# Constant rows of the later q-k buffers by DMA from one small template, at the beginning of an attention and expert kernel

## The chip, the cores and the metric

The kernel runs on one core of one Trainium2 chip. Its time is the device time of one launch in microseconds (us): 778.45 us as the median of three runs (775.94 to 778.54).

## The reference

What is computed is causal attention over 8 batches of 8 heads (576 positions, head size 64) with a bias made of a running sum, and then a layer of eight experts. Each token goes to one expert by a greedy assignment with a capacity of 576 tokens per expert. Cut to what matters:

```python
scores = scale * q @ k.T                      # 8 x 8 heads, 576 x 576
cum    = cumsum(maximum(s, 0))
scores = where(causal, -1e9, scores + minimum(-(cum_i - cum_j), 0))
attn   = exp(scores - max); attn /= attn.sum() + 1e-9
x      = attn @ v                             # 4608 tokens x 512
logits = x @ w_gate                           # 8 experts
# greedy assignment by descending logit, at most 576 tokens for an expert
out[mask_e] = relu(x[mask_e] @ w1[e]) @ w2[e] # for each expert e
```

## The kernel before, in words

The attention works on groups: a group is half the heads of one batch, that is two pairs of heads, and there are 16 groups. A pair is done in three passes on TensorE. The S pass (method `spass`) makes the scores only to find each row's maximum: TensorE writes a tile into one of three `pss` buffers, VectorE adds the mask and takes the maximum (line 471, called a max step below, ten to a pair, each followed by a read of the accumulator). The maxima become two more rows of the q-k buffer: ScalarE and GpSimd split them (lines 518, 520 and 522), TensorE transposes them (524), and a small DMA puts them in place (530). The transposed pass (method `sts`, lines 544 to 547) computes the transposed scores with the maxima subtracted; ScalarE takes the exponential into `P` (555) and GpSimd makes the remainder `R` (557). The third pass multiplies with v (lines 618 to 620).

Numbers are kept as a high and a low half in 16 bits, so a group's q and k need eight copies in a buffer `QK` of 128 partitions. Four such buffers (QK_91 to QK_94 in the instruction lists) are used in turn by the groups 0, 1, 2, 3, 4 and so on. In each, partitions 64 to 69 hold rows for the bias: three that change with the data and come by small DMAs ("aux" rows, line 397), and parts that stay the same in the whole run. These constant rows, and zeros between the halves (lines 297 and 298), are written once per buffer, in `consts`. For buffers 0 and 1 VectorE writes the constant rows (line 285, two instructions for a buffer); buffers 2 and 3 get a copy of buffer 1's by DMA from GpSimd's queue (line 290).

The method `load` brings a group in: four loads of q and k into a `raw` buffer (line 382; two `raw` buffers in turn, 87 and 88), the high half by ScalarE (409), the low half by VectorE (411), moves between partitions by DMA (416), and the aux rows (397). In its list `fresh` stand the waits for the constant rows and zeros of the group's buffer. For group 1 the list also holds `self.moved`, the two DMAs that copy buffer 1's rows.

The order of all instructions is set by a planner (class `Plan`). Each task has an engine, a guessed duration, what it needs, and a priority; the planner plays the program through with its guesses and writes every engine's instructions down in the order that comes out. Each engine then works its list strictly in order, and a waiting instruction holds up all that stand behind it; the DMA issues of the queues SP and GpSimd too. A task with `alt` may go to a second engine.

Before the first group's data is there, TensorE runs 70 matmuls on zeros that nobody reads (line 735, called warm-up below). They stand in its list by priority too, most ahead of the first S pass and the rest between its matmuls.

After the attention follow the router (assignment) and the experts, each with its own plan.

Of the kernel before, what the change touches and what calls it, by code (L numbers as in the profile page):

```python
# [10 lines left out]
F16 = mybir.dt.float16  # L11
# [3 lines left out]
OP = mybir.AluOpType  # L15
# [201 lines left out]
class Attention:  # L217
# [30 lines left out]
    def consts(self):  # L248
        nc, c, pl = self.nc, self.c, self.pl
        g = nc.gpsimd  # L250
        T = lambda shape, dt, name: c.tile(shape, dt, name=name)
        k = self.k = {}
# [19 lines left out]
        for c, v0, rows in ((0, C1, ((5, 0.0), (3, C3), (2, C2), (1, C1))), (1, PSHIFT, ((5, -C1),))):  # L272
            v = self.vec[64:96, c:c + 1]
            P(("vec", c, 0), 0.1, lambda v=v, v0=v0: g.memset(v, v0), -99)
            for n, (below, val) in enumerate(rows):
                P(("vec", c, n + 1), 0.2, lambda v=v, below=below, val=val: g.affine_select(
                    v, v, pattern=[[0, 1]], base=-below, channel_multiplier=1, compare_op=OP.is_ge, fill=val), -99, [("vec", c, n)])
        zrow = self.mZ.bitcast(F16)[64:70, None, 0:HB // 2].to_broadcast([6, 4, HB // 2])
        for i in range(4):
            t = self.r["QK"].slots[i][0]  # L280
            p0 = -97 if i == 0 else 2 * i - 5.6
            rows, made = t[64:70, 0], []
            if i < 2:
                for c in (1, 0):
                    made.append(pl.add("v", 0.85, lambda rows=rows, c=c: nc.vector.tensor_scalar(
                        rows[:, c].rearrange("p r (h c) -> p (r h) c", h=2), zrow, self.vec[64:70, c:c + 1], None,
                        op0=OP.add), [k["vec", 0, 4], k["vec", 1, 1], k["mZ"]], prio=p0 if c or i else -94, lock=True))
            else:

                made.append(pl.add("p", 0.9, lambda rows=rows: nc.gpsimd.dma_start(rows, self.r["QK"].slots[1][0][64:70, 0]),  # L290
                                   self.rows1 + [k["QK", 1]], prio=-20, kb=62))
                self.moved.append(made[0])
            k["row", i] = made
            if i == 1:
                self.rows1, self.moved = made, []
            x = t.rearrange("p a t r c -> p (a t r) c")[:, :, S:OH]
# [66 lines left out]
    def load(self, g):  # L363
# [21 lines left out]
        fresh = [k["QK", g]] if g < 4 else []  # L385
        if g == 1:
            fresh = fresh + self.moved

        if g == 0:
# [15 lines left out]
        for a, z in parts:  # L405
# [3 lines left out]
            hi = [pl.add("a", dur, lambda t=t, a=a, z=z: act(part(A_, 1, t, t, a, z), raw.t[:, t, a:z], AF.Copy, scale=QS),  # L409
                         [ld[r, t] for r in range(a, z)] + fresh[:1], prio=t0 - 5 + off + t / 10, uses=[raw, QK]) for t in range(2)]  # L410
            lo = [pl.add("v", 0.15 + n * S / 960, lambda t=t, a=a, z=z: stt(
# [1060 lines left out]
```

## Time and profile before

| | |
|---|---|
| median of three runs | 778.45 us (775.94 to 778.54) |
| the profiled execution | 777.66 us, of which the span of its instructions 775.6 us |
| TensorE (PE) busy | 722.0 us, 93% of the span |
| VectorE (DVE) busy | 598.2 us, 77% |
| ScalarE (ACT) busy | 391.7 us, 50% |
| GpSimd (POOL) busy | 335.3 us, 43% |
| mean granted clock of TensorE | 0.964 of full |

The shares are averages over stages with different limits: the attention takes about the first 318 us, then the router and the experts. The row of the granted clock in 40 slices shows three places below full speed: slices 2 and 3 of the attention's beginning, slices 17 and 18 between attention and experts, and the last. TensorE's granted clock is given as a share of 2.4 GHz, so 0.5 is 1.2 GHz.

In the rows by windows come, after the stretch and its length, the busy us of PE, PEld (weight loads), DVE, ACT and POOL with the count of instructions, the granted clock (PEclk), the mean busy share of the 16 DMA engines, and GB/s. In a timeline the first number is the start in us from the span's start, the second the time the merged instructions take; in brackets stands how long the engine had been idle before and what released it.

### The profile page before, as it was taken

To read this page: it belongs to the slowest core of one execution; us is meant where nothing else is said; L and a number is where in the kernel's file an instruction comes from. 1 tells how busy PE (TensorE), PEld (TensorE's weight loads), DVE (VectorE), ACT (ScalarE), POOL (GpSimd) and SP (SyncE) were. 2 spreads that over 40 slices of the span, in tenths; PEclk is the share of its full clock that TensorE was granted. 3 is DMA by queue.
4 is the path that set the end of the run, shared out by engine and by line. 5 is a ranking of instruction groups with operands and counts; after the bars stand their busy time and mean duration, and the time that the engine had idled before them with its cause. 6 is when DMAs were issued, how large, how long until landed. Compare 5 with 4: busy or idle time off the path is not lost.

```text
span 775.6 us, 22590 instructions
## 1 busy us (share of the span) xinstructions
PE 722.0 (93%) x8726; PEld 454.9 (59%) x8726; DVE 598.2 (77%) x2014; ACT 391.7 (50%) x794; POOL 335.3 (43%) x428
## 2 busy tenths in 40 slices
PE   9789999999999999628998999999999999999995
PEld 3457788787888888416644544545445454454542
DVE  7889999999999996678895877969788795380110
ACT  3548888888888878405334323324244232461110
POOL 7648988788878988102032041140412224202011
PEclk9679999999999999858999999999999999999998
DMA  7897768686776511106157376394845639851000
GB/s 233 195 213 202 220 175 250 172 241 196 209 203 171 156 35 64 63 35 204 42 167 200 110 113 180 129 222 133 190 156 155 187 105 262 228 180 48 15 28 34
DMA packets 89733, 118.72 MB, mean 153 GB/s; under 512 B 39246, under 2 KB 55758, under 8 KB 89614
## 3 DMA queue, kind: packets, MB, share of 16 engines
q1 hardware_dynamic: 83116, 97.82, 46.1%
q0 software_dynamic: 5952, 19.00, 8.1%
q8 instruction: 68, 1.11, 0.6%
q10 hardware_dynamic: 558, 0.47, 0.2%
q14 instruction: 39, 0.32, 0.1%
HBM read 71.67 MB, written 19.10 MB: 117 GB/s over the span
## 4 chain that ended last, share of the span: by engine, by line
PE 54%; issue 19%; DVE 13%; DMA 5%; POOL 4%; ACT 2%; SPq 1%; POOLq 0%; ACTq 0%; DVEq 0%
PE psm L1293 13%; PE psm L1379 10%; DVE pss L471 5%; PE pst L545 4%; PE pst L544 4%; PE pss L502 3%; PE po L618 3%; PE po L620 2%; PE po L619 2%; POOL out_dram L1352 2%; POOL xg L1226 2%; PE psn L1297 2%; PE po L735 2%; PE pss L681 2%; DMA xg<-xs,ids 1%
## 5 line engine op out<-in xcount | busy, mean ns | idle before, releaser
L557 POOL TENSOR_TENSOR R<-P 128x512 f16<-128x512 f32 (+1 forms) x221 | 218.9, 1016 | 26.9 <-ACT P L555 25.2
L1293 PE MATMUL psm<-xT,w1p 128*128 128x512 f16 (+1 forms) x876 | 193.1, 353 | 1.3 <-DMA xT<-xg 0.8
L1379 PE MATMUL psm<-w2p,hT 128*128 128x512 f16 x768 | 174.4, 379 | 0.0
L555 ACT ACTIVATE P<-pst 128x512 f32<-128x512 f32 (+1 forms) x224 | 119.9, 555 | 25.0 <-PE pst L547 10.3
L1297 PE MATMUL psn<-xT,w1p 128*128 128x64 f16 x768 | 129.7, 193 | 0.0
L471 DVE CUSTOM_DVE_ANT_0 pss<-pss,mS 128x512 f32<-128x512 f32 (+3 forms) x256 | 122.7, 506 | 9.0 <-PE pss L502 8.0
L1293 PEld LDWEIGHTS <-w1p 128*128 128x128 f16 x876 | 79.2, 98 | 80.0 <-issue 1.9
L1352 POOL DMA_INDIRECT out_dram<-y,ids x40 | 39.8, 995 | 198.7 <-ACT y L1390 169.6
L1379 PEld LDWEIGHTS <-hT 128*128 128x128 f16 x768 | 69.0, 98 | 80.3 <-issue 4.4
L1226 POOL DMA_INDIRECT xg<-xs,ids x40 | 43.6, 1089 | 167.3 <-DVE ids L1184 67.3
L618 PE MATMUL po<-V,P 128*128 128x65 f16 x960 | 113.8, 196 | 1.4 <-DVE xp L649 1.0
L620 PE MATMUL po<-V,R 128*128 128x65 f16 x960 | 114.0, 194 | 0.4 <-POOL R L557 0.4
L619 PE MATMUL po<-Vl,P 128*128 128x64 f16 x960 | 113.6, 193 | 0.0
L544 PE MATMUL pst<-QK 70*128 70x64 f16 (+4 forms) x512 | 108.5, 252 | 1.2 <-ACT P L555 0.7
L545 PE MATMUL pst<-QK 128*128 128x64 f16 (+4 forms) x512 | 107.8, 251 | 0.0
L619 PEld LDWEIGHTS <-P 128*128 128x128 bf16 x960 | 90.0, 100 | 9.1 <-issue 2.8
L618 PEld LDWEIGHTS <-P 128*128 128x128 bf16 x960 | 90.4, 98 | 5.9 <-issue 1.8
L1313 ACT ACTIVATE hT<-psm 128x512 f16<-128x512 f32 x64 | 38.2, 597 | 108.1 <-PE psm L1293 88.3
L620 PEld LDWEIGHTS <-R 128*128 128x128 f16 x960 | 89.9, 97 | 0.6 <-POOL R L557 0.6
L1390 ACT ACTIVATE y<-psm 128x512 f32<-128x512 f32 x32 | 19.1, 597 | 122.0 <-PE psm L1379 108.1
L502 PE MATMUL pss<-QK 67*128 67x512 f16 (+3 forms) x256 | 72.6, 307 | 4.7 <-DVE mr L471 2.4
L1297 PEld LDWEIGHTS <-w1p 128*128 128x128 f16 x768 | 67.7, 98 | 1.3
(221 smaller groups left out, 1443.4 us busy)
## 6 DMA issues: line engine op xcount, KB each, us to landing
QK<-QK SPq DMA_DIRECT2D x120, 144.0 KB
wst<-in_w_dram SPq DMA_DIRECT2D x32, 512.0 KB
wst<-in_w_dram SPq DMA_DIRECT2D x64, 256.0 KB
raw<-in_q_dram SPq DMA_DIRECT2D x32, 288.0 KB
raw<-in_k_dram SPq DMA_DIRECT2D x32, 288.0 KB
rv<-in_v_dram SPq DMA_DIRECT2D x32, 288.0 KB
xs<-xp SPq DMA_DIRECT2D x32, 256.0 KB
xs<-xp SPq DMA_DIRECT2D x8, 128.0 KB
```

Source lines behind the costliest of these rows:

```text
L471: return pl.add("v", dur, lambda: nc.vector.tensor_tensor_reduce(ps(), ps(), mask, 1.0, init() if init else -3e38, OP.add, OP.max, mr.t[:, ...
L502: nc.tensor.matmul(ps.t[:, :n], F()[:, q0:q0 + 128], F()[:, k0:k0 + n], start=True, stop=True)
L544: nc.tensor.matmul(ps[:, c0:c0 + n], F()[:, ks:ks + 128], F()[:, q:q + n], start=True, stop=False)
L545: nc.tensor.matmul(ps[:, c0:c0 + n], G()[:, ks:ks + 128], G()[:, q:q + n], start=False, stop=not diag)
L555: e = pl.add("a", n / 1200 + 0.171, lambda: nc.scalar.activation(P.t[:, c0:c0 + n], ps.t[:, :n], AF.Exp, scale=1.0 / YS), [x] + fresh, pri ...
L557: sub = lambda eng: eng.tensor_tensor(R.t[:, c0:c0 + n], P.t[:, c0:c0 + n], strided_hi(P.t)[:, c0:c0 + n], op=OP.subtract)
L618: nc.tensor.matmul(o[:, i], H[:, c:c + 128], V.t[:, pr, sl], start=f, stop=False)
L619: nc.tensor.matmul(o[:, i, 0:64], H[:, c:c + 128], Vl.t[:, pr, sl], start=False, stop=False)
L620: nc.tensor.matmul(o[:, i], R.t[:, c:c + 128], V.t[:, pr, sl], start=False, stop=l)
L1293: nc.tensor.matmul(ps[:, tiles[0]:tiles[-1] + 1] if len(tiles) > 1 else ps[:, tiles[0]], lhs(f, c, a), xT.t[:, tiles[0]:tiles[-1] + 1, 4 * ...
L1297: nc.tensor.matmul(pt.t[:, 64 * f:64 * f + 64], lhs(f, c, a), xT.t[:, 4, 4 * b + c, 0:64], start=s, stop=e)
L1379: nc.tensor.matmul(py.t, hT.t[:, f, a, 128 * i:128 * i + 128], w2p.t[:, f, b], start=f == 0 and k == 0, stop=f == 7 and k == 2)
```

## The change

Only the constants and the loads of the attention are touched. A template tile `rowc` is made: for each of the two kinds of rows 320 columns on six partitions, by one VectorE instruction each. Buffers 1, 2 and 3 get their constant rows from it: two DMAs per buffer on GpSimd's queue, each repeating the 320 columns eight times. The two VectorE instructions that wrote buffer 1's rows are gone, and so are the DMAs that copied them on. The list of group 1 no longer holds the waits for those copies, and the high halves of groups 1 to 3 no longer wait for their buffer's constant rows.

```diff
+        self.rowc = self.c.tile([128, 2, 320], F16, name="rowc")
+        k["rowc"] = [pl.add("v", 0.2, lambda c=c: nc.vector.tensor_scalar(
+            self.rowc[64:70, c], self.mZ.bitcast(F16)[64:70, 0:320], self.vec[64:70, c:c + 1], None, op0=OP.add),
+            [k["vec", 0, 4], k["vec", 1, 1], k["mZ"]], prio=-93, lock=True) for c in (1, 0)]
         for i in range(4):
...
-            if i < 2:
+            if i < 1:
                 for c in (1, 0):
                     made.append(pl.add("v", 0.85, lambda rows=rows, c=c: nc.vector.tensor_scalar(
...
-                made.append(pl.add("p", 0.9, lambda rows=rows: nc.gpsimd.dma_start(rows, self.r["QK"].slots[1][0][64:70, 0]),
-                                   self.rows1 + [k["QK", 1]], prio=-20, kb=62))
-                self.moved.append(made[0])
+                for c in (1, 0):
+                    made.append(pl.add("p", 0.9, lambda rows=rows, c=c: nc.gpsimd.dma_start(
+                        rows[:, c].rearrange("p r (n c) -> p (r n) c", c=320),
+                        self.rowc[64:70, c:c + 1, :].to_broadcast([6, 8, 320])), k["rowc"],
+                        prio=-92 if i == 1 else -20, kb=31))
...
         fresh = [k["QK", g]] if g < 4 else []
-        if g == 1:
-            fresh = fresh + self.moved
...
-                         [ld[r, t] for r in range(a, z)] + fresh[:1], prio=t0 - 5 + off + t / 10, uses=[raw, QK]) for t in range(2)]
+                         [ld[r, t] for r in range(a, z)] + (fresh[:1] if g == 0 else []), prio=t0 - 5 + off + t / 10,
+                         uses=[raw, QK]) for t in range(2)]
```

The planner plays the changed tasks through anew, so the whole attention comes out in another order. Lines below the new ones are numbered two higher after the change.

VectorE, from the low halves of group 0 (QK_91) to the first max steps of its first pair. Before:

```order
L258 MEMSET V_96 128x18
L411 SCALAR_TENSOR_TENSOR QK_91<-raw_87,QK_91 128x576 x4
L285 TENSOR_SCALAR QK_92<-mZ,vec 6x2560
L471 ISA pss_122,mr_105<-pss_122,mS 128x128
L471 ISA mr_105 128x1
```

And after the change:

```order
L258 MEMSET V_97 128x18
L413 SCALAR_TENSOR_TENSOR QK_91<-raw_87,QK_91 128x576 x4
L413 SCALAR_TENSOR_TENSOR QK_92<-raw_88,QK_92 128x2x576 x2
L473 ISA pss_122,mr_105<-pss_122,mS 128x128
L473 ISA mr_105 128x1
```

The constant row of buffer 1 (QK_92) is gone from this place, and the two low halves of group 1, which stood between the max steps of group 0's second pair, now stand ahead of the first max step.

Of TensorE's 70 warm-up matmuls 57 instead of 55 stand ahead of the first S pass.

TensorE, the end of the S pass of group 0's second pair (buffer QK_91). Before, the transposed pass (L544) follows at once:

```order
L502 MATMUL pss_123<-QK_91 128x512
L486 LDWEIGHTS QK_91
L486 MATMUL pss_124<-QK_91 128x512
L486 LDWEIGHTS QK_91
L486 MATMUL pss_124<-QK_91 128x512
L544 LDWEIGHTS QK_91
L544 MATMUL pst_126<-QK_91 128x512
```

After the change matmuls of group 1's S pass (QK_92) stand between, from the first of these rows to the last:

```order
L488 MATMUL pss_124<-QK_91 128x512
L504 LDWEIGHTS QK_92
L504 MATMUL pss_122<-QK_92 128x128
L504 LDWEIGHTS QK_92
L504 MATMUL pss_123<-QK_92 128x256
...
L504 LDWEIGHTS QK_92
L504 MATMUL pss_122<-QK_92 128x256
L546 LDWEIGHTS QK_91
L546 MATMUL pst_126<-QK_91 128x512
```

Seven of the ten tiles of group 1's first pair are now ahead of the transposed pass of group 0's first pair.

GpSimd, from the mask `mU` to the split of the first pair's maxima (mp_110), after the change (before, none of the DMAs and no memset of a QK buffer stood ahead of mp_110):

```order
L261 AFFINE_SELECT mU<-mU 64x64
L295 DMA QK_92<-rowc 6x8x320 x2
L295 DMA QK_93<-rowc 6x8x320 x2
L295 DMA QK_94<-rowc 6x8x320 x2
L301 MEMSET QK_92 128x8x128
L301 MEMSET QK_93 128x8x128
L813 IOTA W 128x8
L301 MEMSET QK_94 128x8x128
...
L828 AFFINE_SELECT tri<-on 128x128
L524 TENSOR_TENSOR mp_110<-ms_108,mp_110 128x10
```

Six DMA issues and three memsets have moved ahead of the router's constants and of mp_110; four selects of the router went behind it.

On SP's queue the moves of group 1 (QK_92) now come ahead of the loads of group 2 (raw_87), which stood before them:

```order
L418 DMA QK_92<-QK_92 64x2x576 x2
L418 DMA QK_91<-QK_91 64x576
L418 DMA QK_92<-QK_92 64x2x576 x2
L442 DMA rv_89<-in_v_dram 128x576
L398 DMA QK_92<-auxk 3x2x576 x2
L418 DMA QK_91<-QK_91 64x576
L386 DMA raw_87<-in_q_dram 128x576
```

Before, all four loads of raw_87 were issued ahead of the first move of QK_92, and its aux rows came after five more issues.

## Rows read from the trace of the kernel before

**Rows 1.** Windows: stretch, length, busy us of PE, PEld, DVE, ACT, POOL, clock, DMA.

```profile
12.00:16.00 4.00, 4.00 (x22) 1.87 (x21) 1.46 (x2) 0.00 (x0) 3.19 (x8) 1.00 0.83 195
16.00:26.50 10.50, 7.19 (x39) 3.11 (x37) 10.05 (x37) 3.96 (x6) 2.48 (x4) 1.00 0.86 245
26.50:36.00 9.50, 7.68 (x57) 4.96 (x55) 7.25 (x14) 6.66 (x12) 6.40 (x7) 0.51 0.90 165
36.00:48.00 12.00, 10.95 (x99) 7.49 (x100) 10.23 (x36) 4.40 (x10) 6.49 (x10) 0.53 0.90 210
48.00:60.00 12.00, 10.38 (x158) 7.37 (x155) 11.09 (x36) 7.71 (x19) 7.04 (x11) 1.00 0.94 226
```

**Rows 2.** Windows of the attention after its beginning.

```profile
60.00:120.00 60.00, 58.65 (x1133) 47.84 (x1131) 59.09 (x195) 51.27 (x122) 50.26 (x56) 1.00 0.72 202
240.00:300.00 60.00, 60.00 (x1198) 49.86 (x1196) 54.85 (x188) 48.79 (x120) 51.59 (x58) 1.00 0.37 109
```

**Rows 3.** Chain of waits, 14 to 37 us: start, us, what.

```profile
21.70 0.88 DVE QK L285
...
26.72 6.87 DMA QK<-QK
33.60 2.46 DMA QK<-auxk
```

**Rows 4.** Timeline of VectorE, 9 to 37 us.

```profile
9.42 0.48 DVE L358 TENSOR_SCALAR xp<-xp 64x576 f16<-64x576 f32 x1
...
12.62 0.88 DVE L285 TENSOR_SCALAR QK<-mZ,vec 6x2560 f16<-6x2560 f16 x1
16.16 0.30 DVE L471 CUSTOM_DVE_ANT_0 pss<-pss,mS 128x128 f32<-128x128 f32 x1 [2.67 <-PE pss L502]
20.89 0.33 DVE L471 CUSTOM_DVE_ANT_0 pss<-pss,mS 128x128 f32<-128x128 f32 x1
24.23 1.35 DVE L444 SCALAR_TENSOR_TENSOR Vl<-rv,V 128x1152 f16<-128x1152 f32 x1
26.11 2.62 DVE L411 SCALAR_TENSOR_TENSOR QK<-raw,QK 128x1152 f16<-128x1152 f32 x2
32.41 1.41 DVE L411 SCALAR_TENSOR_TENSOR QK<-raw,QK 128x1152 f16<-128x1152 f32 x1
36.38 0.30 DVE L471 CUSTOM_DVE_ANT_0 pss<-pss,mS 128x128 f32<-128x128 f32 x1 [2.56 <-PE pss L502]
```

**Rows 5.** Timeline of TensorE, 0 to 48 us.

```profile
1.61 14.34 PE L735 MATMUL po<-mZ 128*128 128x512 f16 x55 [1.61 <-DVE mZ L258]
26.73 0.59 PE L544 MATMUL pst<-QK 70*128 70x512 f16 x1
41.00 1.01 PE L486 MATMUL pss<-QK 67*128 67x512 f16 x2 [0.97 <-DVE mr L471]
```

**Rows 6.** Timeline of GpSimd, 0 to 33 us.

```profile
10.39 2.35 POOL L826 TENSOR_SCALAR_AFFINE_SELECT tri<-on 128x128 f16<-128x128 f16 x1
14.68 0.29 POOL L836 TENSOR_SCALAR_AFFINE_SELECT identf<-identf 128x128 f32<-128x128 f32 x1
21.46 0.21 POOL L522 TENSOR_TENSOR mp<-ms,mp 128x10 f16<-128x10 f32 x1 [6.14 <-ACT ms L520]
22.64 0.95 POOL L297 MEMSET QK<- 128x1024 f16 x1 [0.96 <-DVE QK L285]
23.90 1.32 POOL L290 DMA_DIRECT2D QK<-QK  x2 [0.31 <-POOL QK L297]
29.60 1.84 POOL L297 MEMSET QK<- 128x1024 f16 x2 [4.37 <-DMA QK<-QK]
```

**Rows 7.** Timeline of ScalarE, 29 to 33 us.

```profile
29.27 1.06 ACT L555 ACTIVATE P<-pst 128x512 f32<-128x512 f32 x2
31.47 1.16 ACT L409 ACTIVATE QK<-raw 128x1152 f16<-128x1152 f32 x1
```

**Rows 8.** Page, part 5: GpSimd's costliest DMA issues.

```profile
L1226 POOL DMA_INDIRECT xg<-xs,ids x40 | 43.6, 1089 | 167.3 <-DVE ids L1184 67.3
```

More of the change, by code (lines that the diff above doesn't have):

```diff
@@ L288, in consts @@
             else:
-                made.append(pl.add("p", 0.9, lambda rows=rows: nc.gpsimd.dma_start(rows, self.r["QK"].slots[1][0][64:70, 0]),
-                                   self.rows1 + [k["QK", 1]], prio=-20, kb=62))
-                self.moved.append(made[0])
+                for c in (1, 0):
[3 more added lines that the diff above has]
+                        prio=-92 if i == 1 else -20, kb=31))
             k["row", i] = made
-            if i == 1:
-                self.rows1, self.moved = made, []
             x = t.rearrange("p a t r c -> p (a t r) c")[:, :, S:OH]
```

## The prediction

> **What bounds the kernel now.** The page first: TensorE is busy for 93% of the span, but the row of its granted clock falls below full speed in slices 2 and 3. So I read the windows by stage. From 12 to 16 us TensorE is full, with the warm-up, and VectorE busy for 1.46 of 4 us. From 16 to 26.5 VectorE is the bound: 10.05 of 10.5 us, while TensorE has 7.19. From 26.5 to 48 TensorE is granted 0.51 and 0.53 of its clock, so practically 1.2 GHz, and is busy for 18.63 of 21.5 us; from 48 on it has 2.4 GHz again [rows 1]. The DMA engines have 83 to 94% throughout. Later, from 60 to 120 us, VectorE (59.09 of 60) and TensorE (58.65) are both full, and from 240 to 300 TensorE alone, 60.00 against 54.85 [rows 2]. So a head start at 60 us reaches the end of the attention only if TensorE has it too.
>
> The chain of waits and VectorE's timeline tell why the beginning is slow. VectorE idles 2.67 us before its first max step at 16.16, since TensorE still runs the warm-up that began at 1.61 (55 matmuls, 14.34 us) [rows 4, 5]. Between the max steps of group 0 it then writes a constant row, 0.88 us at 21.70, and makes the low halves of group 1, 2.62 us [rows 3, 4]. After that group 1 isn't there: its moves land only after 6.87 us, its aux rows 2.46 us later [rows 3], and VectorE idles 2.56 us before group 1's first max step at 36.38 [rows 4].
>
> **The change part by part.** The trace gives a price in VectorE's time first.
>
> Removed or moved out of the max steps: the second constant-row instruction, 0.88 us, and the two low halves, 2.62 us [rows 3, 4]. The low halves now fill the idle time before the first max step, where the first constant-row instruction (0.88 us at 12.62) is gone as well: 0.88 + 2.67 = 3.55 us are free there for 2.62 us. VectorE gets some small new work before that: two template instructions of 320 columns and four small memsets that GpSimd had. The trace shows no such template instruction; it is bounded by 0 and the 0.88 us of the row of 2560 columns, and I take 0.25 each, nearer to the small end since it has an eighth of the columns. With about 0.4 for the memsets that makes 0.9 us, and 3.55 - 2.62 = 0.93 us is what the cover has left, with the 0.5 us of the next sentence 1.4. TensorE's list has 57 warm-up matmuls before the first S pass instead of 55; by their mean, 14.34 / 55 = 0.26 us [rows 5], that costs 0.5 us, and the first max step comes at about 16.7.
>
> A pair's ten max steps take 20.89 - 16.16 = 4.73 us [rows 4]. Two pairs end at 16.7 + 9.5 = 26.2, and with the low half of v, 1.35 us, which now follows them, VectorE is free for group 1 at 27.5. If group 1 is there by then, the wait of 2.56 us goes too. On SP's queue five loads of q and k for later groups and two of v that stood ahead of group 1's aux rows now stand behind them, seven of 288 KB, 2.0 MB. At the 165 to 245 GB/s of the windows from 16 to 36 [rows 1] that is 8 to 12 us off the 36.06 at which the aux rows landed (33.60 + 2.46) [rows 3]: 24 to 28. I take 26 to 27, so the wait vanishes, with little to spare. VectorE's sum: 0.88 + 2.62 + 2.56 - 0.5 = 5.6 us.
>
> Now TensorE. In its new list seven of ten tiles of group 1's first pair stand ahead of the transposed pass. They are paced by VectorE's steps, since there are three `pss` buffers; the seventh can start when about half of a pair's steps are done, 2.4 us after 27.5. So the transposed pass begins at 29.9 instead of 26.73 [rows 5]. Those 3.2 us at 1.2 GHz are 1.6 us of full-speed work lost, and 0.9 won by the seven tiles done earlier (2176 columns at 2.4 GHz): 0.7 lost. What it gets back is its idle time: 9.5 - 7.68 = 1.82 and 12 - 10.95 = 1.05 us in the two slow windows, half of it in full-speed work, 1.43, and 12 - 10.38 = 1.62 in the window after [rows 1]. With VectorE ahead by 5.6 us and group 1 there, I count all of it: 3.05 - 0.7 = 2.35 us.
>
> Then the clock. TensorE was idle for 3.3 of the 10.5 us before the clock fell [rows 1], and worked without a stop from about 42 us, after a last wait of 0.97 us [rows 5], until it was granted 2.4 GHz near 48. With the transposed pass, the tiles of group 1 and the third pass all waiting from 29.9 on, I expect an unbroken stretch some us earlier and the clock back with it. Each us of that is half a us of work. I bound it by -2 us (the clock as slow, and 4 us longer) and +5.6 us (back near 37), and take +2.0, 4 us sooner: between the ends, since the fall itself will come again.
>
> TensorE's sum is 2.35 + 2.0 = 4.35 us, below VectorE's 5.6; so TensorE's counts.
>
> Edits that I cost at nothing: GpSimd's six DMA issues and three memsets lie before its first split of maxima. An issue took 1.32 / 2 = 0.66 us and a memset 0.95 [rows 6]; 4 + 2.9 us from about 8.7 on, plus the router's constants up to `tri` (about 5 us, of which `tri` 2.35), end near 21 to 23, and TensorE wants the split only among the last tiles of group 0's second pair, near 25. The cover is some 2 us; the second rival is what happens without it. The longer waits of the high halves that fell away were off the path: ScalarE is busy for 3.96 of 10.5 and 6.66 of 9.5 us [rows 1].
>
> On the price of an issue the rows stand apart. The select `tri` took 2.35 us beside VectorE's low halves, and the same 128 x 128 select 0.29 us when VectorE was idle [rows 6, 4], so a neighbour's work can cost GpSimd 2.06 us per instruction. The Trainium skill, in "SBUF — State Buffer", section "SBUF: two separate sides", says why: a DMA issued from GpSimd needs the ports it shares with VectorE to write its descriptors, and a VectorE instruction in a two-port mode locks it out. By that rule two scaled copies like the one of 0.48 us at 9.42 [rows 4] would hold the issues up, about 1 us in all, which the 2 us of cover take; by the row it could be 6 x 2.06. The two issues of before ran beside max steps, so no row shows which it is.
>
> **The sum.** The profiled execution took 777.66 us, its span 775.6; the 2.06 us around it stay. 777.66 - 4.35 = 773.3 us. The median of the runs shown is 0.8 us above that execution, so the forecast is 774.0 us. A measurement of this kernel can tell about 0.5% from no change, 3.9 us: the border of faster is 774.6.
>
> **The rivals.** *The DMA queue gives it back* (0.27). The bytes are the same, and the engines are already at 83 to 94% [rows 1]. What group 1 gains, group 2's loads lose: four of 288 KB, 1.15 MB, at 200 GB/s some 5.8 us later. ScalarE makes group 2's high halves (before, until 31.47 + 1.16 = 32.6) and in the new list has both ahead of the first exponential, which started at 29.27 [rows 7]. Then the exponentials begin near 33 and TensorE fills three `pst` buffers and waits. For it: ScalarE's strict order; against it: TensorE itself starts only at 29.9 and at 1.2 GHz needs a us for each tile. That would leave 0 to 2 us of gain, 777.4 us, the same.
>
> *GpSimd comes too late* (0.14), the slower side. All six issues and the memsets stand ahead of mp_110 on GpSimd; TensorE's transpose of it stands ahead of the last tiles of group 0 and all of group 1. An issue of 128 rows took 1.09 us [rows 8]; at that price the six cost 2.6 us more and use up the cover. At 0.66 + 2.06 us each they cost 12.4 us more, and the transpose comes 9 to 10 us late, near 35: VectorE then starts group 1 about where it did before, and TensorE has lost most of the 7.68 us that it was busy at 1.2 GHz from 26.5 to 36 [rows 1], say 6.4 us, 3.2 of full-speed work. That makes 777.66 + 3.2 + 0.8 = 781.7 us. It decides from 1 us per issue on. Against it: max steps beside the issues of before did not stretch them.
>
> *The clock hardly falls, or returns at once* (0.07): then VectorE's 5.6 us and more of the idle time count, and the waits on VectorE between 60 and 240 shrink as well; 770 us.
>
> That the change doesn't do what it says I give 0.02: the aux rows still wait for their own buffer's DMAs, but these are issued before 13 us, and a landing took 4.37 us after an issue [rows 6], so 18 us at the latest, long before SP reaches the aux rows.
>
> **How the numbers follow.** The forecast has 0.50, with its own range of 772 to 776.5; about six tenths of it lie below 774.6. Faster: 0.30 + 0.07 + 0.03 from the upper edge of the first rival = 0.40. Slower: 0.14 and 0.02 of reordering for the worse later = 0.16. The same: 0.44. The whole range is 770.0 to 780.0: it takes in the clock's two bounds and the beginning of the late GpSimd, and leaves out its full price.
>
> **What would show it.** Right: VectorE's low halves of group 1 end before its first max step near 16.7; group 1's first max step lies at 27 to 29 instead of 36.38; the first transposed matmul near 30; the windows from 26.5 to 48 show a granted clock above 0.55 and TensorE idle under 1.5 us. Wrong: GpSimd's split of mp_110 after 25, ScalarE waiting for raw loads before its first exponential, or a slow clock that lasts as long as before while the first transposed matmul is late.

## The result and the profile after

The changed kernel took 782.36 us (median of nine executions, 779.75 to 784.12) beside 775.94 us for the kernel before (nine, 773.83 to 778.54): ratio 1.008, 95% interval 1.0065 to 1.0094. The forecast of 774.0 us was wrong, on the wrong side of no change. The profiled execution has a span of 782.4 us, 6.8 us more than before.

First the beginning, in the windows of [rows 1] (same columns), and the middle of the attention in one window:

```profile
12.00:16.00 4.00, 4.00 (x21) 1.76 (x18) 2.70 (x4) 1.18 (x2) 0.96 (x1) 1.00 0.59 55
16.00:26.50 10.50, 7.42 (x33) 3.11 (x32) 6.80 (x24) 1.38 (x2) 4.11 (x13) 0.84 0.82 229
26.50:36.00 9.50, 6.30 (x30) 2.71 (x27) 9.43 (x35) 3.31 (x9) 2.84 (x9) 0.69 0.67 182
36.00:48.00 12.00, 10.11 (x160) 7.47 (x159) 10.65 (x41) 7.63 (x20) 8.62 (x15) 0.96 0.96 251
48.00:60.00 12.00, 11.80 (x191) 9.15 (x189) 10.96 (x42) 10.79 (x25) 11.44 (x12) 1.00 0.88 234
60.00:300.00 240.00, 233.29 (x4491) 190.82 (x4489) 231.55 (x752) 197.05 (x464) 202.75 (x214) 0.99 0.64 178
240.00:270.00 30.00, 26.91 (x515) 21.80 (x514) 29.15 (x87) 20.90 (x50) 23.45 (x23) 0.98 0.47 125
```

The last two windows of the kernel before:

```profile
60.00:300.00 240.00, 237.28 (x4632) 195.63 (x4630) 231.90 (x774) 204.15 (x478) 200.45 (x221) 1.00 0.64 182
240.00:270.00 30.00, 30.00 (x582) 24.53 (x580) 28.71 (x104) 25.05 (x61) 25.75 (x30) 1.00 0.53 154
```

In this profile the beginning was won, though not as planned: by the counts behind the times TensorE ran 414 matmuls from 16 to 60 us, where the same rows of before add up to 353 [rows 1] (405 and 346 in one window, in which a matmul on an inner border counts once). The clock was low for a shorter time: 0.84, 0.69 and 0.96 in the three windows from 16 to 48 us, against 1.00, 0.51 and 0.53. At the 19.3 matmuls per us of the middle (4632 / 240) that is a lead of 3.2 us. This is an estimate, for matmuls differ in size; the columns that they stream, which the trace lists for each, make it 3.5 us. Then, between 60 and 300 us, TensorE stood idle for 6.71 us instead of 2.72, and ran 141 matmuls fewer. Of the 3.99 us of further idle time 3.09 lie from 240 to 270 us, where before it was never idle. There VectorE was busy for 29.15 and 28.71 of 30 us, so nearly full in both. TensorE's two longest waits of that stretch in the timeline of the changed kernel, and one behind them (in brackets the idle time and what ended it):

```profile
262.87 0.19 PE L621 MATMUL po<-Vl,P 128*128 128x64 f16 x1 [0.74 <-DVE Vl L446]
267.86 0.17 PE L694 MATMUL po<-wgp,xt 128*128 128x16 f16 x1 [1.07 <-ACT xp L649]
268.89 0.19 PE L620 MATMUL po<-V,P 128*128 128x65 f16 x1 [0.19 <-DVE xp L651]
```

It waits for the low half of V, then for a copy that ScalarE could make only after VectorE's normalization (L647), which stood behind a low half of 2.15 us. From VectorE's and ScalarE's timelines:

```profile
264.78 2.15 DVE L413 SCALAR_TENSOR_TENSOR QK<-raw,QK 128x1152 f16<-128x1152 f32 x1
267.37 0.44 ACT L649 ACTIVATE xp<-po 128x320 f16<-128x320 f32 x1 [1.89 <-DVE po L647]
```

The end of the attention can be read from the first comparison of the router, a VectorE instruction that stands in the same place in every order. Before:

```profile
321.42 0.68 DVE L971 TENSOR_TENSOR ge<-w,kj 128x1024 f16<-128x1024 bf16 x1
```

After:

```profile
324.94 0.68 DVE L973 TENSOR_TENSOR ge<-w,kj 128x1024 f16<-128x1024 bf16 x1
```

So 3.5 of the 6.8 us were lost by then. The rest came in the experts, where one gather landed late; TensorE waited 4.97 us for it, and its granted clock from 410 to 430 us was 0.83 (before 1.00). TensorE's timeline after, and the window, after and before:

```profile
410.88 0.62 PE L1243 MATMUL psm<-id,xg 128*128 128x128 f16 x8 [0.69 <-DMA xg<-xs,ids]
417.14 1.03 PE L1243 MATMUL psm<-id,xg 128*128 128x128 f16 x8 [4.97 <-DMA xg<-xs,ids]
```

```profile
410.00:430.00 20.00, 14.34 (x96) 7.06 (x96) 7.20 (x25) 5.90 (x9) 4.92 (x9) 0.83 0.73 167
410.00:430.00 20.00, 18.30 (x160) 9.64 (x161) 13.49 (x40) 8.84 (x15) 1.97 (x3) 1.00 0.59 165
```

### The profile page after: what moved, and what is told of

It reads as the page before. It is cut to its first block, busy times and chain, and to the rows that moved or that the text cites. A ratio compares the mean times of both kernels' runs of the same rounds, so it can differ in the third digit from the quotient of the medians.

```text
span 782.4 us, 22588 instructions
## 1 busy us (share of the span) xinstructions
PE 723.0 (92%) x8726; PEld 453.7 (58%) x8726; DVE 602.0 (77%) x2019; ACT 390.3 (50%) x794; POOL 342.9 (44%) x427
## 4 chain that ended last, share of the span: by engine, by line
PE 36%; issue 18%; DVE 4%; POOL 4%; DMA 2%; ACT 1%; POOLq 0%; SPq 0%; ACTq 0%; DVEq 0%
PE psm L1295 13%; PE psm L1381 11%; POOL out_dram L1354 2%; PE psn L1299 2%; PE psa L1003 1%; POOL xg L1228 1%; DMA xg<-xs,ids 1%; PE pst L547 1%; PE pst L546 1%; DVE ge L973 1%; PE po L620 1%; PE psm L1378 1%; PE psm L1374 1%; PE po L622 1%; PE po L621 1%
## 5 line engine op out<-in xcount | busy, mean ns | idle before, releaser
L559 POOL TENSOR_TENSOR R<-P 128x512 f16<-128x512 f32 (+1 forms) x220 | 222.8, 1039 | 30.9 <-ACT P L557 27.7
L547 PE MATMUL pst<-QK 128*128 128x64 f16 (+4 forms) x512 | 106.0, 249 | 0.0
```

Of the source, the lines that this page charges most:

```text
L547: nc.tensor.matmul(ps[:, c0:c0 + n], G()[:, ks:ks + 128], G()[:, q:q + n], start=False, stop=not diag)
L559: sub = lambda eng: eng.tensor_tensor(R.t[:, c0:c0 + n], P.t[:, c0:c0 + n], strided_hi(P.t)[:, c0:c0 + n], op=OP.subtract)
```

## The experiments

They ran in five batches, each batch on a chip of its own with the kernel before beside it, which took 771.9 to 773.5 us: e1 to e4, e5 to e8, e9 to e12, e13 to e16, and e17 with e18. The ratios compare within a batch; profiles of different batches, e8 and e17 among them, come from different chips. Eight (e1 to e7 and e18) fix the order by a table: in place of the planner's `run`, which picks the next task, the tasks are started as the table lists them, and each engine's list follows. The line numbers of such a kernel are some 20 higher.

```diff
-        self.pl.run()
+        self.pl.replay()
+    def replay(self):
+        todo = [(self.all[z[:-1]], z[-1]) for z in ORDER.split()]
+        while todo:
+            for n, (x, e) in enumerate(todo):
+                t = None if x.left else self._when(x, e)
+                if t is not None:
+                    break
+            todo.pop(n)
+            self.start(t, x, e)
```

What all runs gave, with TensorE's busy time out of the 240 us from 60 to 300, and the start of the router's first comparison (one profile each):

| run | ratio to before, 95% | busy, us | router, us |
|---|---|---|---|
| e8 before, again | (one execution) | 237.42 | 319.61 |
| e17 after, again | 1.0085 (1.0068 to 1.0101) | 233.65 | 324.88 |
| e4 new instructions, old order | 1.0009 (0.9995 to 1.0022) | 237.59 | 319.42 |
| e2 old instructions and start, new order from 60 us | 1.0080 (1.0051 to 1.0108) | 233.34 | 327.61 |
| e1 new start, old order from 60 us | 1.0039 (1.0021 to 1.0057) | 235.87 | 321.14 |
| e18 new order to 140 us, then old | 1.0095 (1.0078 to 1.0112) | 233.26 | 325.32 |
| e3 after, batch late | 1.0154 (1.0130 to 1.0178) | 234.85 | 327.10 |
| e7 after, two moves | 1.0083 (1.0059 to 1.0107) | 233.75 | 325.11 |
| e9 before, no low half of V | 0.9939 (0.9919 to 0.9959) | 239.47 | 315.38 |
| e10 after, no low half of V | 1.0016 (0.9999 to 1.0033) | 235.82 | 320.22 |
| e11 after, V's low half unlocked | 1.0178 (1.0150 to 1.0206) | 229.90 | 331.31 |
| e12 after, low halves sooner | 1.0078 (1.0055 to 1.0100) | 234.43 | 324.52 |
| e13 before, 0.88 for 0.85 us | 1.0052 (1.0026 to 1.0077) | 232.51 | 323.45 |
| e14 before, 1.2 for 1.1 us | 1.0037 (1.0017 to 1.0057) | 234.29 | 322.17 |
| e15 after, 0.6 for 0.9 us | 1.0083 (1.0055 to 1.0111) | 233.26 | 327.09 |
| e16 after, 1.2 for 1.1 us | 1.0091 (1.0067 to 1.0114) | 233.44 | 327.42 |
| e5 before, four more DMAs | 1.0056 (1.0034 to 1.0077) | 237.07 | 323.80 |
| e6 as e4, old number of DMAs | 1.0024 (1.0008 to 1.0040) | 237.41 | 323.76 |

A profile shows one execution. That of e4 is the fastest of its twelve (770.73 us, median 773.29); those of e5 and e15 are the slowest of their six (780.81 and 783.75 us, medians 776.41 and 780.10).

**Instructions or order.** e1 and e2 exchange the order at 60 us of the planner's time, e4 puts the new instructions into the old order.

```diff
 # e1: ORDER = after's tasks with a planned start below 60 us, then the remaining ones as before has them
 # e2: the kernel before; ORDER = before's tasks below 60 us, then the remaining ones as after has them
 # e4: ORDER = before's; rowc ahead of buffer 0's rows, the DMAs where the rows of buffers 1 to 3 stood
```

> The changed kernel's instructions and order for what the planner starts before its own 60 us, and from there the order of the kernel before on every engine (a table holds the order). Theory A (the beginning is won, and the loss lies in the order that the planner wrote for the middle of the attention): no hole in TensorE at 245 to 275 us, the attention ends some 3 us sooner than before, 772.5 us, ratio to before 0.994 to 0.998. Theory B (what the beginning wins is taken back later whatever the order, because VectorE has no slack or the clock falls again): 776 us or more, ratio 1.000 or above, with idle time of TensorE somewhere between 60 and 300 us.

> The mirror image: the instructions and the order of the kernel before for its first 60 planned us, and from there the order of the changed kernel. Theory A: the beginning as slow as before, and the hole of 5 to 6 us at 245 to 275 us with its clock loss as in the changed kernel, so slower than both: 782 to 786 us, ratio 1.008 to 1.013. Theory B (the loss comes of the new beginning): no hole, 776 us, ratio 1.000.

> The instructions of the change without the order that it brought: the template and the DMAs stand where the rows stood in the order of the kernel before, and everything else keeps that order on every engine, the second group's first cast behind the rows included. Theory A: VectorE loses two row instructions of 0.88 us and gets two of 0.3 us, nothing else moves, no hole: 774.5 to 776.5 us, ratio 0.998 to 1.001. Rival (the DMAs of the constant rows themselves cost something that the trace doesn't put down to them): 778 us or more, ratio 1.003 or above.

e4 came out the same as before, in time and at the router's first comparison (319.42 against 319.61 us): by themselves the instructions neither cost nor win anything that can be measured (the interval ends at 1.0022). e2 has none of them, and an old beginning, and is as slow as the changed kernel, with the same three waits:

```profile
267.24 0.19 PE L640 MATMUL po<-Vl,P 128*128 128x64 f16 x1 [0.74 <-DVE Vl L465]
272.23 0.17 PE L713 MATMUL po<-wgp,xt 128*128 128x16 f16 x1 [1.08 <-ACT xp L668]
273.26 0.19 PE L639 MATMUL po<-V,P 128*128 128x65 f16 x1 [0.19 <-DVE xp L670]
```

So the order of the middle makes the loss: that half of Theory A is shown. Its other half, that the won beginning would last, fell with e1, slower than before although its order from 60 us on is the old one. From 65 to 80 us TensorE was busy for 13.32 of 15 us in e1, where the kernel before has all 15.00:

```profile
65.00:80.00 15.00, 13.32 (x236) 10.32 (x233) 14.34 (x42) 11.12 (x26) 14.04 (x15) 1.00 0.82 230
```

**What in that order.** e3 and e7 take single suspects out of the hole.

```diff
 # e3: the ten VectorE tasks of the router's first batch moved ahead of its second batch
 # e7: V's low half of 261.5 us ahead of the low half of 258.2 us; the low half of 264.8 us behind the normalization
```

> The changed kernel in its own order, but ten VectorE instructions of the router's first batch (they run from 236 to 257 us in the changed kernel and take 5.7 us there) stand after 280 us, ahead of the second batch. Theory A1 (the batch, which the new order put at a stretch where VectorE is 98% busy, is what makes the low half of V late): the low half that starts at 261.5 us comes before TensorE wants it, the 3.3 us of idle time and the 3.4 us of half clock behind it are gone, 777 us, ratio 1.000 to 1.003. Rival A2 (VectorE is late there for other reasons, the low halves bunched at 258 to 274 us): the hole stays and the time is that of the changed kernel, 782 us, ratio 1.008.

> The changed kernel in its own order with two VectorE instructions moved: the low half of V that starts at 261.5 us stands ahead of the low half of q or k that starts at 258.2 us, and the low half that starts at 264.8 us (2.15 us long, between the reciprocal and the multiply of one normalization) stands behind that normalization. Theory A3 (the hole at 260 to 275 us is the order of these few VectorE instructions): TensorE's waits of 0.74 and 1.07 us and the half clock behind them go, the attention ends 3 to 5 us sooner than in the changed kernel, ratio to before 1.001 to 1.004. Rival (VectorE as a whole is behind there, any order waits): the idle time turns up within 15 us at another instruction, ratio 1.007 to 1.009.

Both suspects fell. In e3 the waits of the hole stayed (0.71 and 1.08 us), and the batch at its new place made TensorE wait near the end of the attention. In e7 the two waits were gone, and another of 1.41 us stood in their stead:

```profile
307.88 0.21 PE L642 MATMUL po<-V,P 128*128 128x65 f16 x1 [3.73 <-DVE xp L673]
```

```profile
263.10 0.22 PE L548 MATMUL pss<-ident,mp 128*128 128x128 f16 x1 [1.41 <-DVE mr L495]
```

The first line is e3, the second e7; e7's ratio of 1.0083 is what its rival said. My next theory was that the lead of TensorE is a debt of VectorE: e9 and e10 relieve VectorE in both kernels, e11 and e12 have the planner make the low halves sooner.

```diff
 # e9 (before), e10 (after)
-            Vl.t, rv.t, VS, V.t[:, :, :, 0:64], op0=OP.mult, op1=OP.subtract), [hi], ...
+            Vl.t, 0.0) if g < 3 else None, [hi], ...        # nc.vector.memset
 # e11 (after), V's low half
-prio=t0 - 2, uses=[rv, V, Vl], lock=True)
+prio=t0 - 2, uses=[rv, V, Vl])
 # e12 (after): low halves of q and k t0 - 4.6 -> t0 - 5.6; V t0 - 2 -> t0 - 3; V's high half t0 - 1.2 -> t0 - 2.2
```

> The kernel before in its own order without V's low half: 13 of the 16 VectorE instructions of 1.35 us that make it are left out and the first three are replaced by a memset to zero, so V is carried by its high half alone; TensorE's matmuls are all there. For comparison with the next run. VectorE, 9.5 of 10 us busy in the middle of the attention, is relieved by 17.6 us, TensorE was busy there already: the attention ends 0 to 3 us sooner, ratio to before 0.996 to 1.000.

> The changed kernel in its own order with the same left out (V's low half). Theory F (the new order lets TensorE run 3 us ahead while VectorE is two to three low halves, 2.7 to 4 us, further behind than before at the same TensorE work, and this debt is called in at 245 to 275 us): with VectorE relieved no debt is called in, the lead of the beginning lasts to the attention's end, and the run is 2 to 4 us faster than the run of before with the same left out, ratio to before 0.991 to 0.997. Rival G (the hole at 245 to 275 us is a matter of how the new order places instructions on several engines, whatever VectorE's load): the hole stays, the run is 3 to 6 us slower than its partner, ratio to before 1.002 to 1.008.

> The changed kernel whose planner no longer keeps V's low half away from times at which GpSimd computes (one word in its call); the order follows from the planner again. By the planner's own times the low halves that stand done at 160 us of TensorE work rise from 31 to 34 (33 in the kernel before), and the lead of 4 us over before lasts to the attention's end instead of shrinking to 1.5 us. Theory F: no hole at 245 to 275 us, the attention ends 1 to 3 us sooner than before, ratio 0.996 to 1.000, though each low half that meets GpSimd takes up to 2.1 us. Rival G: a hole somewhere in the attention all the same, ratio 1.004 to 1.009.

> The changed kernel whose planner gives the low halves of q, k and V, and V's high half, priorities one group-half earlier (1.0 less), the lock kept. By the planner's own times 32 low halves stand done at 160 us of TensorE work (31 in the changed kernel) and the lead of 4 us lasts to 3.5 us at the end. Theory F: between the changed kernel and before, with half of the debt called in: ratio 0.999 to 1.004. Rival G: 1.004 to 1.009.

Theory F fell. e9 gained more than I expected, 0.6%, and e10 stayed 1.0016 / 0.9939 = 1.008 behind it, the same ratio as with V's low half, so rival G held. The wait for V is gone in e10, of course; the one for ScalarE's copy stands where it stood:

```profile
264.30 0.17 PE L694 MATMUL po<-wgp,xt 128*128 128x16 f16 x1 [0.82 <-ACT xp L649]
```

e11 was the worst of all: V's 16 low halves, no longer kept apart from GpSimd's work, took 1.48 us in the median instead of 1.35, 1.6 us more in all, and TensorE was idle for 10 us, so the longer instructions alone don't explain it. e12 was no better than the changed kernel.

**A bad middle or any new middle.** e13 to e16 change one number that the planner is told and no instruction.

```diff
 # e13 (before), the row instructions
-made.append(pl.add("v", 0.85, lambda rows=rows, c=c: nc.vector.tensor_scalar(
+made.append(pl.add("v", 0.88, lambda rows=rows, c=c: nc.vector.tensor_scalar(
 # e14 (before) and e16 (after)
-k["QK", i] = pl.add("p", 1.1, lambda x=x: g.memset(x, 0.0), made, prio=p0 + 0.1,
+k["QK", i] = pl.add("p", 1.2, lambda x=x: g.memset(x, 0.0), made, prio=p0 + 0.1,
 # e15 (after), the row DMAs
-made.append(pl.add("p", 0.9, lambda rows=rows, c=c: nc.gpsimd.dma_start(
+made.append(pl.add("p", 0.6, lambda rows=rows, c=c: nc.gpsimd.dma_start(
```

> The kernel before; the planner is told 0.88 us, in place of 0.85, for one row instruction of VectorE (0.88 is what the trace shows). The instructions are the same, and the order is redrawn from the first 20 us on: about two thirds of VectorE's instructions keep their sequence, as between the kernels before and after. Theory H (the old order is a lucky draw, and any redraw costs 4 to 7 us in the middle of the attention): ratio 1.004 to 1.010. Rival I (the new beginning of the change makes the bad middle): ratio 0.997 to 1.002.

> The kernel before; the planner is told 1.2 us, in place of 1.1, for the memset of a q-k buffer's columns on GpSimd. Instructions the same, order redrawn (three quarters of VectorE's sequence kept). Theory H: ratio 1.004 to 1.010. Rival I: 0.997 to 1.002.

> The changed kernel; the planner is told 0.6 us, in place of 0.9, for GpSimd's time to issue one of the row DMAs (the trace of the changed kernel shows 0.6). Order redrawn. Theory H: the middle is another draw, 65 to 305 us costs 9 to 15 us of TensorE time in place of 15.3, ratio to before 1.000 to 1.010, and the loss sits at another place than 245 to 275 us. Rival I: the same hole, ratio 1.006 to 1.010.

> The changed kernel; the planner is told 1.2 us, in place of 1.1, for the memset of a q-k buffer's columns. Order redrawn. Theory H: as the run before it, ratio 1.000 to 1.010, with its loss at a place of its own. Rival I: the same hole, 1.006 to 1.010.

Theory H held, with e14 just below its range: 30 ns in one guess make the kernel before 0.5% slower. e13, from its windows:

```profile
16.00:60.00 44.00, 39.58 (x481) 25.91 (x479) 41.52 (x142) 27.51 (x59) 29.69 (x45) 0.88 0.73 197
60.00:300.00 240.00, 232.51 (x4467) 190.21 (x4464) 229.70 (x751) 197.19 (x461) 203.22 (x210) 0.99 0.65 183
```

and the same windows of e8, the kernel before again (on another chip than e13):

```profile
16.00:60.00 44.00, 37.36 (x356) 23.65 (x355) 40.73 (x124) 25.04 (x51) 25.29 (x34) 0.77 0.81 216
60.00:300.00 240.00, 237.42 (x4648) 196.05 (x4648) 231.76 (x773) 203.82 (x477) 200.57 (x221) 1.00 0.64 183
```

At 60 us e13 is 125 matmuls ahead, at 19.3 per us 6.5 us (5.7 by columns), more than the change ever won, with the old instructions; at the router it is 3.8 us behind. The holes lie elsewhere in each draw: in e15 and e16 TensorE waits for V's low half at 284.8 and 286.1 us (0.58 and 0.80 us, in e15 with a clock of 0.94 from 240 to 300), in e13 for a DMA of q-k rows at 134.7 us (1.75 us). In the old order no wait between 60 and 300 us is longer than 0.62 us.

**The lead and the rest.** e17 and e8 are the two kernels unchanged; e18 hands over to the old order at 140 us.

```diff
 # e18: ORDER = after's tasks with a planned start below 140 us, then the remaining ones as before has them
```

> The kernel before, unchanged, for a profile from the same chip as the runs beside it: the attention's end within 0.3 us of the first profile of it (Theory A: that part is set by the order and repeats), the experts' part up to 3 us off (their gathers don't repeat).

> The changed kernel, unchanged, on the chip of the other runs. The hole at 245 to 275 us repeats, since the order fixes it (waits of 0.7 us on V's low half and of 1.07 us on ScalarE's copy), the attention ends 3 to 5 us later than in the repeated run of before; the experts' part differs from the first profile by up to 3 us, as it did between two profiles of before. Ratio 1.007 to 1.010.

> The changed kernel in its own order for what its planner starts before 140 us, and from there in the order of before. Theory H1 (the lead is real and the loss is only the hole of the new order): the lead of 3 us survives, no hole, ratio 0.995 to 0.999, faster than both. Rival (the lead of TensorE is one over VectorE and the loads, which at the same TensorE work stand 3 us behind those of the old order at 140 us by the planner's list, so the old order makes TensorE wait where it takes over): 2 to 4 us of idle time within 20 us of 140 us, ratio 1.000 to 1.005.

In e17 the waits of 0.74, 1.07 and 0.19 us repeat to the hundredth, as its expectation said. The router starts 5.3 us later than in e8, of 5.6 us between the spans (776.1 and 770.5): on this pair, which is of two chips, nearly nothing is lost behind the attention, and next to nothing was won in the beginning (368 matmuls from 16 to 60 us, e8 356; by columns e17 is 0.2 us behind). In e8 I was wrong: the attention ended 1.8 us off the first profile, not 0.3. e18 lost its lead where the old order took over, as the rival said, and its ratio of 1.0095 is above the 1.000 to 1.005 that the rival reckoned:

```profile
157.12 0.22 PE L548 MATMUL pss<-ident,mp 128*128 128x128 f16 x1 [3.66 <-DVE mr L495]
```

**GpSimd's DMAs.** The changed kernel's loss behind the attention made me suspect the queue that its row DMAs share with the gathers.

```diff
 # e5 (before, its own order), behind the two row DMAs
+if i == 3:
+    for n in range(4):
+        idle = self.dr.tile([7, 8, 320], F16, name=f"idle{n}")
+        pl.add("p", 0.9, lambda idle=idle: nc.gpsimd.dma_start(
+            idle, self.mZ.bitcast(F16)[64:71, None, 0:320].to_broadcast([7, 8, 320])), [k["mZ"]], kb=36)
 # e6: as e4, but buffer 1's rows by nc.scalar.dma_start, those of buffers 2 and 3 copied from buffer 1
```

> The kernel before in its own order, with four more GpSimd DMAs of 56 packets each (zeros to memory that nothing reads) behind the two that it has there: as many as the change adds. The runs with the change's instructions lost some 3 us between the end of the attention and the end of the kernel. Theory C (GpSimd's further DMAs, which go through the queue of the later gathers, cost the experts those 3 us): ratio 1.003 to 1.005. Theory D (the experts' time moves with the moment at which their gathers meet the weight loads, and not with those DMAs): ratio 0.999 to 1.001.

> As the run with the change's instructions alone in the old order, but the second buffer's rows come from the template by two DMAs of ScalarE's queue, and the rows of the last two buffers are copied from the second by GpSimd as in the kernel before: GpSimd issues two DMAs, as before. The attention should end some 2 us sooner than before in either case. Theory C: nothing is lost behind it, ratio 0.996 to 0.998. Theory D: the experts take it back as in the run with the instructions alone, ratio 1.000 to 1.002.

The ratio of e5 lies above Theory C's range, and its interval overlaps it. Its profile, that of the slowest execution, splits the loss against e8 in two. The router starts 4.2 us late, while TensorE's middle is as good as ever (237.07): this part is lost in the beginning, 328 matmuls from 16 to 60 us where e8 has 356, and its cause isn't known. Another 4.1 us are lost behind the router (455.1 us from there to the end, e8 450.9), as Theory C has it, with a late gather like that of the changed kernel:

```profile
415.79 1.03 PE L1267 MATMUL psm<-id,xg 128*128 128x128 f16 x8 [4.67 <-DMA xg<-xs,ids]
```

But e4 and e17, which issue as many DMAs on GpSimd's queue, take 449.1 and 451.2 us behind the router. So the DMAs alone don't cost the experts 3 us each time. e6, with the old count of DMAs, is no faster than e4 with the new. It doesn't show D either, for e6 lost in its beginning as well (320 matmuls).

## Why the prediction was wrong, step by step

- **VectorE's 5.6 us.** Group 1's first max step came at 31.86 instead of 36.38 [rows 4], 4.5 us sooner; 27 to 29 would have been 7 to 9. The first max step was late (18.03, not 16.7). ScalarE had stood idle for 2.83 us ahead of its second cast of group 1, and VectorE then for 1.74, so that its low halves ended at 17.8. But TensorE set the time: its first tile of the S pass started at 17.66, after 1.29 us of waiting for a DMA, and the max step followed 0.37 us later, as it had before (15.79 and 16.16). The sum has no such wait; the other five profiles with this beginning show it too, 1.02 to 1.97 us. Then the first pair's ten max steps took 26.01 - 18.03 = 8.0 us instead of the 4.73 of the prediction, for VectorE waited four times for TensorE's tiles, up to 1.23 us, while seven warm-up matmuls took 2.50 us, 0.36 each instead of 0.26 (the clock of that window is 0.84). From the timelines of VectorE, ScalarE and TensorE after, and in the last line TensorE's of before:

```profile
16.44 1.36 DVE L413 SCALAR_TENSOR_TENSOR QK<-raw,QK 128x1152 f16<-128x1152 f32 x1 [1.74 <-ACT QK L410]
18.03 0.30 DVE L473 CUSTOM_DVE_ANT_0 pss<-pss,mS 128x128 f32<-128x128 f32 x1 [0.23 <-POOL W L813]
21.86 0.30 DVE L473 CUSTOM_DVE_ANT_0 pss<-pss,mS 128x128 f32<-128x128 f32 x1 [1.23 <-PE pss L504]
26.01 0.33 DVE L473 CUSTOM_DVE_ANT_0 pss<-pss,mS 128x128 f32<-128x128 f32 x1
31.86 0.29 DVE L473 CUSTOM_DVE_ANT_0 pss<-pss,mS 128x128 f32<-128x128 f32 x1
15.24 1.16 ACT L410 ACTIVATE QK<-raw 128x1152 f16<-128x1152 f32 x1 [2.83 <-DVE QK L413]
25.52 1.17 ACT L444 ACTIVATE V<-rv 128x1152 f16<-128x1152 f32 x1 [9.12 <-DVE mr L473]
34.70 1.16 ACT L410 ACTIVATE QK<-raw 128x1152 f16<-128x1152 f32 x1 [2.57 <-DMA raw<-in_k_dram]
35.77 1.07 ACT L557 ACTIVATE P<-pst 128x512 f32<-128x512 f32 x2
17.66 0.22 PE L504 MATMUL pss<-QK 67*128 67x128 f16 x1 [1.29 <-DMA rv<-in_v_dram]
18.89 0.43 PE L504 MATMUL pss<-QK 67*128 67x256 f16 x2 [1.01 <-DMA QK<-xp]
19.21 2.50 PE L737 MATMUL po<-mZ 128*128 128x512 f16 x7
34.08 0.63 PE L546 MATMUL pst<-QK 70*128 70x512 f16 x1
47.08 0.23 PE L526 MATMUL pss<-ident,mp 128*128 128x128 f16 x1 [1.59 <-POOL mp L524]
15.79 0.49 PE L502 MATMUL pss<-QK 67*128 67x128 f16 x3
```

- **TensorE's 2.35 us of idle time.** Not won: the transposed pass began at 34.08, not near 30, and TensorE was idle for 3.20 + 1.89 = 5.09 us in the two windows from 26.5 to 48, where I wanted under 1.5 and before had 2.87 [rows 1]. Of the 1.89 us one wait for GpSimd's split of maxima at 47.08 makes 1.59. Only the window behind, from 48 to 60, went as reckoned: 0.20 us instead of 1.62. From 16 to 60 us TensorE was idle for 8.37 us in all, before for 7.80.
- **The clock's 2.0 us.** Right in sign and too small. Clock times length from 16 to 48 us gives 0.84 x 10.5 + 0.69 x 9.5 + 0.96 x 12 = 26.9 us of full speed on offer, before 10.5 + 0.51 x 9.5 + 0.53 x 12 = 21.7: 5.2 us more, near my upper bound of 5.6. The lead of 3.2 us is less than that: the idle time is 0.6 us longer, and the rest isn't accounted for.
- **The first rival's mechanism came, and not its result.** ScalarE did wait for group 2's raw loads, 2.57 us ahead of 34.70, and the first exponential began at 35.77 (29.27 before [rows 7]; the rival said 33). But it came 1.69 us behind the first transposed matmul (34.08), and up to 60 us TensorE's longest wait for ScalarE was 0.19 us.
- **The second rival didn't come.** Its 781.7 us lie near the measured time by chance. GpSimd's six issues took 0.83 + 2.84 us, 0.61 each. Its first split of maxima at 26.97, later than the 25 that I named, waited for ScalarE's, and that for the first pair's last max step, which began at 25.34; ScalarE's cast of V (25.52 to 26.69) stood in between. What GpSimd did wait for was the landing of the rows before two memsets, 2.45 and 1.59 us. By the rule of the Trainium skill ("SBUF — State Buffer", section "SBUF: two separate sides") the issues could have been held up beside VectorE. The first took 0.83 us and the other five 0.57 each, where before it was 0.66 [rows 6], so a hold-up of more than 0.3 us isn't there. GpSimd's timeline after:

```profile
7.98 0.83 POOL L295 DMA_DIRECT2D QK<-rowc  x1 [1.09 <-DVE rowc L280]
9.15 2.84 POOL L295 DMA_DIRECT2D QK<-rowc  x5 [0.34 <-DVE rowc L280]
14.44 0.96 POOL L301 MEMSET QK<- 128x1024 f16 x1 [2.45 <-DMA QK<-rowc]
16.98 0.96 POOL L301 MEMSET QK<- 128x1024 f16 x1 [1.59 <-DMA QK<-rowc]
26.97 0.21 POOL L524 TENSOR_TENSOR mp<-ms,mp 128x10 f16<-128x10 f32 x1 [5.81 <-ACT ms L522]
```

- **The step that failed.** The sum ended at 60 us. I wrote that a head start at 60 us reaches the end of the attention only if TensorE has it too, and then took that condition for enough; the 240 us behind it had no term, and "reordering for the worse later" a chance of 0.02. But the planner had written every engine's list anew there. The one term that the sum had, 4.35 us, was too large as well. The beginning gave 3.2 us on the first pair and 0.6 on the second (e17 against e8, 12 matmuls). Over the six profiles that begin as the changed kernel does (after, e1, e3, e7, e17 and e18: 405, 395, 399, 370, 368 and 393 matmuls in one window from 16 to 60 us) the mean is 388, over the three that begin as before does (before, e2 and e8: 346, 351 and 356) it is 351: some 1.9 us. And the new middle took more. From 60 us to the router the first pair lost 3.2 + 3.5 = 6.7 us, the second 0.6 + 5.3 = 5.9; 3.99 and 3.77 us of that are further idle time of TensorE, and the rest, matmuls that came slower, isn't traced. e4 and e2 show that this is the order and not the instructions; e13 and e14, that the old order loses it as well when it is drawn anew.

Open remain two things. What makes the old order good isn't found: the batch, two misplaced low halves and V's low half are each ruled out as the whole cause, and e1 and e18 say only that its later part can't be joined to another beginning for nothing. Nor is it known how the old order came about, and so whether a redraw must cost something: no run shows it. And the 3.3 us behind the attention in the first profile, with 0.83 of the clock, didn't repeat in e17, whose ratio is the same. In the twenty profiles TensorE waited over 2 us for a gather between 395 and 430 us in four, with the changed kernel's count of GpSimd's DMAs in three (after 4.97, e15 3.81, e5 4.67) and the old count in one (e6 2.88); what makes it late stays open. No run beat the kernel before with all of the work in it.

## What to carry to other kernels

Where a planner or scheduler lays out the code, an edit at the beginning changes the whole list: compare the lists far behind the edit, and give the redraw a term of its own. Seven redraws here (after, e11 to e16) cost 0.4 to 1.8%, more than the edit was worth. Before judging an edit, separate the two: put the new instructions into the old order, and redraw the old order by a slight change of a guess that touches no instruction.

## What was not expected of the hardware

The three waits at 262 to 271 us repeat to 0.01 us from one profile of the changed kernel to another, but the beginning doesn't: of the kernel before the router's first comparison started at 321.42 us in one profile and at 319.61 in a later one, with the same mean clock of 0.77 from 16 to 60 us in both, and 346 and 356 matmuls in that window. The six profiles that begin as the changed kernel does differ by up to 37 matmuls there, 1.9 us, with clocks of 0.81 to 0.88, and e17 and e18, on one chip, by 25, 1.3 us. So one profile doesn't give the first 60 us to better than some 2 us, half of what I had set out to predict.
